# Linear attention and a gated MLP on one core: the heads of a pair on the two partition halves, v padded with zeros

## The chip, the cores and the metric

One core of a Trainium2 chip runs the whole program in one launch. The metric is device time in microseconds (us). An engine's instructions run in the order in which they stand in its own queue; the engines wait for each other through semaphores.

## The reference

For each of 4 sequences and 8 heads a state of 48 x 48 numbers is carried over 768 steps; the output of the heads, side by side, goes through a gated MLP whose gate mixes over time.

```python
for t in range(S):
    cur = einsum('bhd,bhe->bhde', u * k[t], v[t])
    y[t] = einsum('bhd,bhde->bhe', r[t], state + cur)
    state = w * state + einsum('bhd,bhe->bhde', k[t], v[t])
h = relu(x @ w_in);  u, v = h[..., :512], h[..., 512:]
v_s = einsum('ts,bsd->btd', w_spatial, layernorm(v)) + b_spatial
out = (u * v_s) @ w_out
```

## The kernel before, in words

**Attention.** A sequence is cut into 6 chunks of 128 steps, 24 chunks in all, numbered m. Inside a chunk the recurrence becomes matrix products: scores k x r (masked so that a step sees only earlier ones, with the u term on the diagonal) times v, plus the state at the chunk's start times r. A chunk has two halves of 64 steps, z = 0 and 1, each with its own decay reference, so the state is carried from half to half. The 8 heads form 4 pairs p of two heads j.

- `load_chunk` (L84) issues two loads on SP's queue: `rk` (r and k with the head dimension on the partitions, 64 for each head of a pair, L90) and `rkv` (r, k and v with time on the partitions, L94). In `rkv` v has 64 columns for each head, 48 of them filled. Three buffers of each exist.
- `prep` (L236) scales: `scale` (L247, L248, L250) multiplies r and k by powers of w, `rku` (L253, L254) forms r k u, `ks` (L257) scales k with the table `tn`, `red` (L260) sums r k u over a head, `dia` (L269) writes these sums onto the diagonal of the chunk's score tile `a`.
- `g1` (L278) on TensorE: for each head and half, k x r into the PSUM tile `ps` (L286, 16 matmuls with 64 rows and 64 columns), then k x v (L295, 16 such matmuls, 48 wide; 8 ahead of the last chunk of a sequence, since only the first half's is needed there). `ps` has two banks. The row half from which a matmul reads decides its bank.
- `mid` (L305): VectorE copies the scores into `a` under the mask (L309) and carries the state on (L317, L322, L324, L325); ScalarE copies the state into block-diagonal tiles `sb`, 128 rows for a pair of heads (L302, L303).
- `g2` (L328) on TensorE into `xp`: state x r as 12 matmuls for each half (24 in all, 12 in a sequence's first chunk), each with 128 rows of contraction and 32 columns, cycling over the four groups of 32 output partitions; then a x v as 32 matmuls with 64 rows and 32 columns, one for each half, part of a head and output group. All go through `mm` (L335).
- `fin` (L357) splits the result into a high and a low part, `xh` (ScalarE, L365) and `xl` (VectorE, L367).

**MLP.** Each product of the MLP runs as three matmuls of split values (`mm3`, L391 to L393): `moe_v` (L397), `moe_u` (L453), `moe_sp` (L464, the mixing over time), `moe_out` (L478). Weights arrive as 64-bit floats and are unpacked and split by VectorE and ScalarE in small pieces (`from_f64`, lines 182 to 202).

**Order.** Every engine's queue is in the order of the Python code. The main loop runs over chunks i: g2 and fin of chunk i, g1 and mid of chunk i + 1, the loads of chunk i + 3, then `prep` of chunk i + 2 mixed with MLP steps and, in the first chunks, with pieces of weight unpacking (the tables `FIRST` and `POUR` say how many). So TensorE sees for each chunk a dense group of small fp32 matmuls (state x r, a x v, scores, k x v) and then a long run of MLP matmuls. An fp32 matmul of the program appears in the trace as two weight loads and two matmuls, a matmul of the MLP as one of each.

Of the kernel before, what the change touches and what calls it, by code (L numbers as in the profile page):

```python
# [32 lines left out]
ROW = OV + H * 64  # L33
# [3 lines left out]
def fused_kernel(ctx, tc, rkT, rkvN, wT, uB, w_in, w_sp, b_sp, w_out, out):  # L37
# [4 lines left out]
    KPOOL, DACT, VPOOL = 7, 0, 2  # L42
    XPE, SPE = 0, 0
# [89 lines left out]
    mask = const.tile([P, HC], F32, name="mask")  # L133
    nc.gpsimd.memset(mask, 1.0)
    nc.gpsimd.affine_select(out=mask[64:P], in_=mask[64:P], pattern=[[-1, 64]], compare_op=ALU.is_gt,
                            fill=0.0, base=0, channel_multiplier=1)
    nc.gpsimd.affine_select(out=mask[0:64], in_=mask[0:64], pattern=[[1, 64]], compare_op=ALU.is_gt,
                            fill=0.0, base=0, channel_multiplier=-1)
    nc.scalar.mul(neg, eye, -1.0)
    mask_u = mask.bitcast(U32)  # L140
    tn = const.tile([P, NP, 2, D], F32, name="tn")
# [4 lines left out]
    tn_f = tn.rearrange("s p j d -> s (p j d)")  # L146
# [59 lines left out]
    rests = []  # L206

    def sp_pieces(t, j):
        def f():
            if t * NS + j < SPE:  # L210
                hi, lo = (w[:, j, t * TH:(t + 1) * TH] for w in (ws_h, ws_l))
                pm = ps_m.tile([P, 512], F32, name="pm")[:, 0:TH]
                nc.tensor.matmul(pm, eye, raws["sp", t, j], start=True, stop=False)
                nc.scalar.copy(hi, raws["sp", t, j])

                def rest():
                    nc.tensor.matmul(pm, neg, hi, start=False, stop=True)
                    nc.scalar.copy(lo, pm)

                rests.append(rest)  # L220
                if len(rests) > 1:
                    rests.pop(0)()
                if j == NS - 1 or t * NS + j == SPE - 1:
                    rests.pop(0)()
                return
# [10 lines left out]
    def prep(m):  # L236

        rk, rkv = dmas.pop(m)
        rn, kn = rkv[:, 0:DM], rkv[:, OK:OK + DM]
# [4 lines left out]

        def scale():
            if m < KPOOL:
                nc.gpsimd.tensor_tensor(out=rk[:, 1], in0=rk[:, 1], in1=tt, op=ALU.mult)  # L247
# [4 lines left out]
        def rku():
            nc.gpsimd.tensor_tensor(out=rn, in0=rn, in1=kn, op=ALU.mult)  # L253
            nc.gpsimd.tensor_tensor(out=rn, in0=rn, in1=ub, op=ALU.mult)  # L254

        def ks():
            nc.gpsimd.tensor_tensor(out=kn, in0=kn, in1=tn_f, op=ALU.mult)  # L257

        def red():
            nc.vector.tensor_reduce(out=dg.rearrange("s j p -> s p j"),  # L260
                                    in_=rn.rearrange("s (p j d) -> s p j d", p=NP, j=2), axis=AX.X, op=ALU.add)

        def dia():
            if m < DACT:
                for j in range(2):
                    for p in range(NP):
                        nc.scalar.mul(a[:, j, p, :], diag, dg[:, j, p:p + 1])
            else:
                nc.gpsimd.tensor_tensor(out=a.rearrange("s j p t -> s (j p) t"),  # L269
                                        in0=diag.unsqueeze(1).to_broadcast([P, H, HC]),  # L270
                                        in1=dg.rearrange("s j p -> s (j p)").unsqueeze(2).to_broadcast([P, H, HC]),
                                        op=ALU.mult)
# [5 lines left out]
    def g1(m):  # L278
        t = at[m]
        ps = ps_a.tile([P, 2, 512], F32, name="ps")  # L280
        t["ps"] = ps
        for p in range(NP):
            for j in range(2):
                for z, s0, t0 in SUBS:
                    hd = slice(64 * j, 64 * j + 64)
                    nc.tensor.matmul(ps[s0:s0 + 64, j, p * HC:(p + 1) * HC], t["k"][hd, p, s0:s0 + 64],  # L286
                                     t["r"][hd, p, t0:t0 + 64], start=True, stop=True, skip_group_check=True)
        for p in range(NP):
            for j in range(2):
                for z, s0, t0 in SUBS:  # L290
                    if z == 1 and m % NC == NC - 1:
                        continue
                    h = 2 * p + j
                    e0 = 0 if j == 0 else 16
                    nc.tensor.matmul(ps[64 * j:64 * j + 64, s0 // 64, 256 + p * D:256 + (p + 1) * D],  # L295
                                     t["kn"][s0:s0 + 64, h * D:h * D + 64], t["v"][s0:s0 + 64, h, e0:e0 + D],
                                     start=True, stop=True, skip_group_check=True)
# [7 lines left out]
    def mid(m):  # L305
        t, c = at[m], m % NC
        ps = t["ps"]
        ua, ub_ = (ps[:, i, 256:256 + NP * D].rearrange("p (n e) -> p n e", n=NP) for i in (1, 0))
        nc.vector.copy_predicated(out=t["a"], mask=mask_u.unsqueeze(1).unsqueeze(1).to_broadcast([P, 2, NP, HC]),  # L309
                                  data=ps[:, :, 0:256].rearrange("s j (p t) -> s j p t", p=NP))  # L310
        if c == 0:
            block(sblk[1], ua)
            t1 = ua
        else:
# [2 lines left out]
            nc.vector.tensor_tensor(out=t1, in0=st["s"], in1=ua, op=ALU.add)  # L317
            block(sblk[1], t1)
        if c < NC - 1:
            if c == 0:  # L320
                t1 = sm.tile([P, NP, D], F32, name="t1", bufs=1)
# [4 lines left out]
            st["s"] = s2

    def g2(m):  # L328
# [5 lines left out]
        def mm(z, g, jt, lhsT, rhs):  # L334
            nc.tensor.matmul(xp[32 * g:32 * g + 32, z, jt * HC:(jt + 1) * HC], lhsT, rhs, start=(z, g) not in began,  # L335
                             stop=True, skip_group_check=True, tile_position=(ROWP[0], 32 * g))
# [9 lines left out]
        parts = []  # L346
        for jt, g, p, k in quads:
            if k < 2:
                parts.append((jt, g, p, 0, 32 * k))
            if k > 0:  # L350
                parts.append((jt, g, p, 1, 32 * (k - 1)))
        for jt, g, p, j, e in parts:
            for z, s0, t0 in SUBS:
                ROWP[0] = s0
                mm(z, g, jt, t["v"][s0:s0 + 64, 2 * p + j, e:e + 32], t["a"][s0:s0 + 64, j, p, :])

    def fin(m):  # L357
# [11 lines left out]
        return xs, xl, xh, src

    def fin_low(m, xl, xh, src):

        if m < XPE:
            for z in range(2):
                nc.tensor.matmul(src[:, z], neg, xh[:, z], start=False, stop=True, skip_group_check=True)
            nc.scalar.copy(xl, src)

# [253 lines left out]
```

## Time and profile before

| what | value |
|---|---|
| median of 3 runs | 379.26 us (378.18 to 381.27) |
| profiled execution: its own time is the span from first to last instruction | 378.2 us, 1.1 us below the median |
| mean granted TensorE clock | 0.973 |
| TensorE matmul busy | 337.6 us (89%), 5436 instructions |
| weight loads busy | 311.0 us (82%), 5436 instructions |
| VectorE / ScalarE / GpSimd busy | 212.1 / 140.7 / 158.9 us |
| DMA | 41.67 MB |

In the profile PE is TensorE's matmul, PEld its weight load, DVE VectorE, ACT ScalarE, POOL GpSimd and SP the queue that issues the loads. A row of a timeline has the start, the time, the engine, the line, the operation, output <- input, the shapes, how many instructions are merged, and in brackets how long the engine was idle before and what ended that. A row of a group has its busy time, the mean of one in ns, and the idle time before. A row of waits has the total, the number of times and the longest. A row of stretches has the length and then each engine's busy time with its number of instructions, the clock, the DMA share and GB/s. "issue" is a wait for nothing that the profile shows. Matmuls overlap, so their busy time is longer than what they cost; the distance from start to start is what one costs.

### The profile page before, as it was taken

The numbers are of one execution on the slowest core, as the hardware profiler recorded it, in microseconds if no ns is written. First come the engines' busy times: TensorE is split into PE (matmuls) and PEld (weight loads), VectorE is DVE, ScalarE is ACT, GpSimd is POOL, SyncE is SP. The second block draws the span as 40 slices with busy tenths as digits, with TensorE's granted clock in tenths as the row PEclk, the third lists the DMA queues.
The fourth block names the chain that finished last, engine by engine and source line by source line (L and its number), as shares of the span: only waits on it lengthen the run. The fifth ranks groups of instructions, "written<-read, shape, count | busy, mean of one in ns | idle before, by whom it ended". The sixth has DMA issues, their size and how long they took to land.

```text
span 378.2 us, 12232 instructions
## 1 busy us (share of the span) xinstructions
PE 337.6 (89%) x5436; PEld 311.0 (82%) x5436; DVE 212.1 (56%) x419; ACT 140.7 (37%) x310; POOL 158.9 (42%) x162
## 2 busy tenths in 40 slices
PE   2456693997999998998999899999999999999995
PEld 1445472886999997988989899889999998999994
DVE  6698997598655444384444444587444533443120
ACT  3036125747213323647123223547123334461212
POOL 6764854844345271564643263241554330003120
PEclk9996987898999999999999999999999999999999
DMA  7994932450304314323214214333032010000101
GB/s 260 416 390 149 340 103 92 141 178 21 129 2 157 126 74 154 127 67 127 65 35 157 94 56 171 127 117 127 13 110 83 3 44 23 2 0 2 42 21 62
DMA packets 14020, 41.67 MB, mean 110 GB/s; under 512 B 1680, under 2 KB 6416, under 8 KB 13968
## 3 DMA queue, kind: packets, MB, share of 16 engines
q1 hardware_dynamic: 13968, 40.90, 30.7%
q8 instruction: 42, 0.69, 0.8%
q14 instruction: 10, 0.08, 0.1%
HBM read 36.18 MB, written 4.72 MB: 108 GB/s over the span
## 4 chain that ended last, share of the span: by engine, by line
PE 75%; DVE 11%; ACT 4%; DMA 3%; issue 3%; POOL 2%; SPq 0%; POOLq 0%; ACTq 0%; DVEq 0%
PE pm L391 21%; PE pm L393 20%; PE pm L392 20%; PE xp L335 8%; PE ps L286 3%; PE ps L295 2%; DMA wst<-w_sp 2%; DMA rkv<-rkvN 2%; DVE a L309 1%; DVE rk L248 1%; ACT vs L435 1%; DVE q L412 1%; DVE pm L198 1%; DVE pm L194 1%; ACT vnorm L437 1%
## 5 line engine op out<-in xcount | busy, mean ns | idle before, releaser
L473 POOL TENSOR_TENSOR g<-g,u 128x384 f32<-128x384 f32 x32 | 32.6, 1018 | 118.5 <-DVE g L472 118.5
L391 PE MATMUL pm<-ws_h,vnorm 128*128 128x384 f32 x192 | 64.9, 338 | 0.0
L393 PE MATMUL pm<-ws_h,vnorm 128*128 128x384 f32 x192 | 64.3, 335 | 0.0
L392 PE MATMUL pm<-ws_l,vnorm 128*128 128x384 f32 x192 | 64.2, 334 | 0.0
L269 POOL TENSOR_TENSOR a<-diag,dg 128x512 f32<-128x512 f32 x24 | 25.6, 1067 | 67.6 <-DVE dg L260 40.8
L172 DVE TENSOR_TENSOR gt<-g,gt 128x384 fp32r<-128x384 f32 x32 | 20.9, 654 | 58.2 <-ACT gt L171 58.2
L171 ACT CAST gt<-g 128x384 fp32r<-128x384 f32 x32 | 16.4, 514 | 90.5 <-POOL g L473 90.5
L393 PE MATMUL pm<-xh,wi_l 128*128 128x384 f32 x96 | 33.7, 351 | 5.0 <-DVE wi_l L202 5.0
L391 PE MATMUL pm<-xh,wi_h 128*128 128x384 f32 x96 | 34.3, 358 | 3.6 <-ACT u L461 2.4
L391 PEld LDWEIGHTS pm<-ws_h,vnorm 128*128 128x128 f32 x192 | 36.0, 188 | 0.3
L392 PEld LDWEIGHTS pm<-ws_l,vnorm 128*128 128x128 f32 x192 | 36.0, 188 | 0.0
L393 PEld LDWEIGHTS pm<-ws_h,vnorm 128*128 128x128 f32 x192 | 36.0, 188 | 0.0
L391 PE MATMUL pm<-wo_h,gt 128*128 128x384 f32 x96 | 33.0, 344 | 0.8 <-ACT gt L171 0.8
L392 PE MATMUL pm<-xl,wi_h 128*128 128x384 f32 x96 | 33.3, 347 | 0.0
L393 PE MATMUL pm<-wo_h,gt 128*128 128x384 f32 x96 | 32.4, 337 | 0.0
L392 PE MATMUL pm<-wo_l,gt 128*128 128x384 f32 x96 | 32.3, 336 | 0.0
L335 PEld LDWEIGHTS xp<-rk,sb 128*32 128x32 f32 x1056 | 18.0, 115 | 16.4 <-issue 8.4
L335 PE MATMUL xp<-rk,sb 128*32 128x64 f32 x1056 | 23.4, 232 | 8.7 <-DVE xl L367 6.3
L391 PE MATMUL pm<-wi_h,xh 128*128 128x512 f32 x72 | 29.7, 412 | 0.6 <-DVE wi_l L202 0.6
L472 DVE TENSOR_TENSOR g<-pm,bb 128x384 f32<-128x384 f32 x32 | 17.7, 553 | 21.3 <-PE pm L393 21.2
L392 PE MATMUL pm<-wi_l,xh 128*128 128x512 f32 x72 | 29.0, 403 | 0.0
L393 PE MATMUL pm<-wi_h,xl 128*128 128x512 f32 x72 | 28.7, 398 | 0.0
(87 smaller groups left out, 691.9 us busy)
## 6 DMA issues: line engine op xcount, KB each, us to landing
rkv<-rkvN SPq DMA_DIRECT2D x24, 648.0 KB, 5.7
rk<-rkT SPq DMA_DIRECT2D x24, 512.0 KB, 4.3
out<-ob SPq DMA_DIRECT2D x24, 192.0 KB, 1.9
raw<-w_in SPq DMA_DIRECT2D x6, 512.0 KB, 9.9
wst<-w_sp SPq DMA_DIRECT2D x12, 192.0 KB, 5.9
raw<-w_out SPq DMA_DIRECT2D x4, 384.0 KB, 6.9
bb<-b_sp SPq DMA_DIRECT2D x1, 384.0 KB, 5.6
ub<-uB SPq DMA_DIRECT2D x1, 192.0 KB, 6.6
```

Of the source, the lines that this page charges most:

```text
L171: nc.scalar.copy(hi, src)
L172: (eng or nc.vector).tensor_tensor(out=lo, in0=src, in1=hi.bitcast(F32), op=ALU.subtract)
L194: nc.vector.scalar_tensor_tensor(out=z["w"], in0=raws[key][:, :, 0], scalar=2.0 ** -52, in1=z["w"], op0=ALU.mult, op1=ALU.mult)
L269: nc.gpsimd.tensor_tensor(out=a.rearrange("s j p t -> s (j p) t"), in0=diag.unsqueeze(1).to_broadcast([P, H, HC]), in1=dg.rearrange("s j p ...
L286: nc.tensor.matmul(ps[s0:s0 + 64, j, p * HC:(p + 1) * HC], t["k"][hd, p, s0:s0 + 64], t["r"][hd, p, t0:t0 + 64], start=True, stop=True, sk ...
L295: nc.tensor.matmul(ps[64 * j:64 * j + 64, s0 // 64, 256 + p * D:256 + (p + 1) * D], t["kn"][s0:s0 + 64, h * D:h * D + 64], t["v"][s0:s0 + ...
L335: nc.tensor.matmul(xp[32 * g:32 * g + 32, z, jt * HC:(jt + 1) * HC], lhsT, rhs, start=(z, g) not in began, stop=True, skip_group_check=Tru ...
L391: nc.tensor.matmul(o, lh, rh, start=first, stop=False)
L392: nc.tensor.matmul(o, lh, rl, start=False, stop=False)
L393: nc.tensor.matmul(o, ll, rh, start=False, stop=last)
L472: nc.vector.tensor_tensor(out=g, in0=pm[:, 0:TH], in1=bb[:, ts_], op=ALU.add)
L473: nc.gpsimd.tensor_tensor(out=g, in0=g, in1=u, op=ALU.mult)
```

## The change

- The two heads of a pair no longer share the partitions of `ps` and `a`: one head's scores lie on partitions 0 to 63, the other's on 64 to 127, for both time halves z. Which head lies on which half alternates with p (`j ^ b`, b = p // 2), so that in each partition half the two row halves write to different banks.
- v is loaded once for each time half, with 96 columns for a pair; in the rows of a head, the columns of the other head are zeros. `rkv` grows from 1296 to 1552 floats on each partition, 648 to 776 KB.
- a x v becomes, for each half z, 12 matmuls with 128 rows and 32 columns over both heads of a pair: 24 in place of 32.
- `g1` has the same number of matmuls with the same shapes, in another order and at other places of `ps`.
- The mask, the table `tn`, the reduction, the diagonal, the copies and the state's walk through `ps` follow the new layout; `tn` is made by 16 matmuls of 64x48 in place of 4 transposes, the mask by four selections in place of two; `eye` moves into a scratch tile, and `neg`, which only unused branches read, is gone with these (their switches, `XPE`, `SPE` and `DACT`, were 0).

```diff
-ROW = OV + H * 64
+VB = 2 * D
+ROW = OV + 2 * NP * VB
...
-    eye = const.tile([P, P], F32, name="eye")
-    neg = const.tile([P, P], F32R, name="neg")
+    eye = tmp[:, 384:384 + P]
...
-    mask = const.tile([P, HC], F32, name="mask")
+    mask = const.tile([P, 2, HC], F32, name="mask")
...
+    for hf in range(2):
+        for z, sign in ((0, -1), (1, 1)):
+            m_ = mask[64 * hf:64 * hf + 64, z]
+            nc.gpsimd.affine_select(out=m_, in_=m_, pattern=[[sign, 64]], compare_op=ALU.is_gt,
+                                    fill=0.0, base=0, channel_multiplier=-sign)
...
-        nc.tensor.transpose(pt[:, 0:P], tt[:, p, :], eye)
-        nc.scalar.copy(tn[:, p, :, :], pt[:, 0:P].rearrange("s (j d) -> s j d", j=2)[:, :, 0:D])
+        for z, p2, hf in ((z, p2, hf) for z in range(2) for p2 in range(2) for hf in range(2)):
...
+            nc.tensor.matmul(pt[64 * hf:64 * hf + 64, (2 * p2 + z) * D:(2 * p2 + z + 1) * D],
+                             tt[hd, 2 * b + p2, c0:c0 + 64], eye[hd, 64 * j:64 * j + D], start=True, stop=True,
+                             skip_group_check=True)
+        nc.scalar.copy(tn[:, b], pt[:, 0:4 * D])
...
-        for p in range(NP):
-            for j in range(2):
-                for z, s0, t0 in SUBS:
-                    hd = slice(64 * j, 64 * j + 64)
-                    nc.tensor.matmul(ps[s0:s0 + 64, j, p * HC:(p + 1) * HC], t["k"][hd, p, s0:s0 + 64],
-                                     t["r"][hd, p, t0:t0 + 64], start=True, stop=True, skip_group_check=True)
...
-                    nc.tensor.matmul(ps[64 * j:64 * j + 64, s0 // 64, 256 + p * D:256 + (p + 1) * D],
-                                     t["kn"][s0:s0 + 64, h * D:h * D + 64], t["v"][s0:s0 + 64, h, e0:e0 + D],
-                                     start=True, stop=True, skip_group_check=True)
+        quad = [(p2, z, s0, t0, j, b) for p2 in range(2) for z, s0, t0 in SUBS for b in range(2) for j in range(2)]
+        for p2, z, s0, t0, j, b in quad:
+            hd, hf, p, o = slice(64 * j, 64 * j + 64), j ^ b, 2 * b + p2, (2 * p2 + z) * HC
+            nc.tensor.matmul(ps[64 * hf:64 * hf + 64, b, o:o + HC], t["k"][hd, p, s0:s0 + 64],
+                             t["r"][hd, p, t0:t0 + 64], start=True, stop=True, skip_group_check=True)
+        for p2, z, s0, t0, j, b in quad:
+            if z == 1 and m % NC == NC - 1:
+                continue
+            hs, p, o = slice(64 * (j ^ b), 64 * (j ^ b) + 64), 2 * b + p2, 256 + (2 * z + p2) * D
+            kc = (4 * b + 2 * p2 + z) * D
+            nc.tensor.matmul(ps[64 * j:64 * j + 64, b, o:o + D], t["kn"][hs, kc:kc + 64],
+                             t["v"][hs, z, p, j * D:(j + 1) * D], start=True, stop=True, skip_group_check=True)
...
-        nc.vector.copy_predicated(out=t["a"], mask=mask_u.unsqueeze(1).unsqueeze(1).to_broadcast([P, 2, NP, HC]),
-                                  data=ps[:, :, 0:256].rearrange("s j (p t) -> s j p t", p=NP))
+        nc.vector.copy_predicated(out=t["a"].rearrange("s b q z t -> s (b q) (z t)"),
+                                  mask=mask_u.rearrange("s z t -> s (z t)").unsqueeze(1).to_broadcast([P, 4, P]),
+                                  data=ps[:, :, 0:256].rearrange("s b (q c) -> s b q c", q=2))
...
-        parts = []
-        for jt, g, p, k in quads:
-            if k < 2:
-                parts.append((jt, g, p, 0, 32 * k))
-            if k > 0:
-                parts.append((jt, g, p, 1, 32 * (k - 1)))
-        for jt, g, p, j, e in parts:
-            for z, s0, t0 in SUBS:
-                ROWP[0] = s0
-                mm(z, g, jt, t["v"][s0:s0 + 64, 2 * p + j, e:e + 32], t["a"][s0:s0 + 64, j, p, :])
+        for z in range(2):
+            for jt, g, p, k in quads:
+                mm(z, g, jt, t["v"][:, z, p, 32 * k:32 * k + 32], t["a"][:, p // 2, p % 2, z, :])
```

More of the change, by code (lines that the diff above doesn't have):

```diff
@@ L41, in fused_kernel @@
         ctx.enter_context(tc.manual_schedule(engines={e}))
-    KPOOL, DACT, VPOOL = 7, 0, 2
-    XPE, SPE = 0, 0
+    KPOOL, VPOOL = 7, 2
     FIRST = [0, 0, 1, 3, 6, 10]
@@ L132, in fused_kernel @@
     nc.gpsimd.tensor_tensor(out=diag, in0=eye[:, 0:64], in1=eye[:, 64:P], op=ALU.add)
-    mask = const.tile([P, HC], F32, name="mask")
+    mask = const.tile([P, 2, HC], F32, name="mask")
     nc.gpsimd.memset(mask, 1.0)
[L135 to L139, printed above, removed]
+    for hf in range(2):
[3 more added lines that the diff above has]
+                                    fill=0.0, base=0, channel_multiplier=-sign)
     mask_u = mask.bitcast(U32)
-    tn = const.tile([P, NP, 2, D], F32, name="tn")
-    for p in range(NP):
+    tn = const.tile([P, 2, 2 * 2 * D], F32, name="tn")
+    for b in range(2):
         pt = ps_m.tile([P, 512], F32, name="pm")
-        nc.tensor.transpose(pt[:, 0:P], tt[:, p, :], eye)
-        nc.scalar.copy(tn[:, p, :, :], pt[:, 0:P].rearrange("s (j d) -> s j d", j=2)[:, :, 0:D])
-    tn_f = tn.rearrange("s p j d -> s (p j d)")
+        for z, p2, hf in ((z, p2, hf) for z in range(2) for p2 in range(2) for hf in range(2)):
+            j = hf ^ b
+            hd = slice(64 * j, 64 * j + 64)
+            c0 = 64 if z == 0 else 0
+            nc.tensor.matmul(pt[64 * hf:64 * hf + 64, (2 * p2 + z) * D:(2 * p2 + z + 1) * D],
+                             tt[hd, 2 * b + p2, c0:c0 + 64], eye[hd, 64 * j:64 * j + D], start=True, stop=True,
+                             skip_group_check=True)
+        nc.scalar.copy(tn[:, b], pt[:, 0:4 * D])
+    tn_f = tn.rearrange("s b c -> s (b c)")
     atiles = []
     for n in range(2):
-        t = const.tile([P, 2, NP, HC], F32, name=f"a{n}")
+        t = const.tile([P, 2, 2, 2, HC], F32, name=f"a{n}")
         nc.gpsimd.memset(t, 0.0)
@@ L204, in from_f64 @@
         return [first, high, power, low, add, rest]
-    rests = []
     def sp_pieces(t, j):
         def f():
[L210 to L225, printed above, removed]
             split(ws_h[:, j, t * TH:(t + 1) * TH], ws_l[:, j, t * TH:(t + 1) * TH], raws["sp", t, j])
@@ L240, in prep @@
         a = atiles[m % 2]
-        dg = sm.tile([P, 2, NP], F32, name="dg")
+        dg = sm.tile([P, H], F32, name="dg")
         at[m] = dict(r=rk[:, 0], k=rk[:, 1], kn=rkv[:, OK:OK + DM + 16],
-                     v=rkv[:, OV:ROW].rearrange("s (h e) -> s h e", h=H), a=a)
+                     v=rkv[:, OV:ROW].rearrange("s (z p e) -> s z p e", z=2, p=NP), a=a)
         def scale():
@@ L259, in red @@
         def red():
-            nc.vector.tensor_reduce(out=dg.rearrange("s j p -> s p j"),
-                                    in_=rn.rearrange("s (p j d) -> s p j d", p=NP, j=2), axis=AX.X, op=ALU.add)
+            nc.vector.tensor_reduce(out=dg, in_=rn.rearrange("s (h d) -> s h d", h=H), axis=AX.X, op=ALU.add)
         def dia():
-            if m < DACT:
-                for j in range(2):
[L266 to L272, printed above, removed]
+            nc.gpsimd.tensor_tensor(out=a.rearrange("s b q z t -> s (b q z) t"),
+                                    in0=diag.unsqueeze(1).to_broadcast([P, H, HC]),
+                                    in1=dg.unsqueeze(2).to_broadcast([P, H, HC]), op=ALU.mult)
         return [scale, lambda: (rku(), ks()), red, dia]
@@ L281, in g1 @@
         t["ps"] = ps
-        for p in range(NP):
-            for j in range(2):
-                for z, s0, t0 in SUBS:
-                    hd = slice(64 * j, 64 * j + 64)
-                    nc.tensor.matmul(ps[s0:s0 + 64, j, p * HC:(p + 1) * HC], t["k"][hd, p, s0:s0 + 64],
-                                     t["r"][hd, p, t0:t0 + 64], start=True, stop=True, skip_group_check=True)
-        for p in range(NP):
-            for j in range(2):
-                for z, s0, t0 in SUBS:
[L291 to L295, printed above, removed]
-                                     t["kn"][s0:s0 + 64, h * D:h * D + 64], t["v"][s0:s0 + 64, h, e0:e0 + D],
-                                     start=True, stop=True, skip_group_check=True)
+        quad = [(p2, z, s0, t0, j, b) for p2 in range(2) for z, s0, t0 in SUBS for b in range(2) for j in range(2)]
[10 more added lines that the diff above has]
+                             t["v"][hs, z, p, j * D:(j + 1) * D], start=True, stop=True, skip_group_check=True)
     st = {}
     def block(dst, src):
-        nc.scalar.copy(dst[0:64, :, 0:D], src[0:64])
-        nc.scalar.copy(dst[64:P, :, D:2 * D], src[64:P])
+        d4 = dst.rearrange("p (b q) e -> p b q e", b=2)
+        nc.scalar.copy(d4[0:64, :, :, 0:D], src[0:64])
+        nc.scalar.copy(d4[64:P, :, :, D:2 * D], src[64:P])
     def mid(m):
@@ L307, in mid @@
         ps = t["ps"]
-        ua, ub_ = (ps[:, i, 256:256 + NP * D].rearrange("p (n e) -> p n e", n=NP) for i in (1, 0))
-        nc.vector.copy_predicated(out=t["a"], mask=mask_u.unsqueeze(1).unsqueeze(1).to_broadcast([P, 2, NP, HC]),
-                                  data=ps[:, :, 0:256].rearrange("s j (p t) -> s j p t", p=NP))
+        ua, ub_ = (ps[:, :, 256 + z * 2 * D:256 + (z + 1) * 2 * D].rearrange("p b (q e) -> p b q e", q=2)
+                   for z in range(2))
+        nc.vector.copy_predicated(out=t["a"].rearrange("s b q z t -> s (b q) (z t)"),
+                                  mask=mask_u.rearrange("s z t -> s (z t)").unsqueeze(1).to_broadcast([P, 4, P]),
+                                  data=ps[:, :, 0:256].rearrange("s b (q c) -> s b q c", q=2))
         if c == 0:
@@ L315, in mid @@
             block(sblk[0], st["s"])
-            t1 = sm.tile([P, NP, D], F32, name="t1", bufs=1)
+            t1 = sm.tile([P, 2, 2, D], F32, name="t1", bufs=1)
             nc.vector.tensor_tensor(out=t1, in0=st["s"], in1=ua, op=ALU.add)
@@ L320, in mid @@
             if c == 0:
-                t1 = sm.tile([P, NP, D], F32, name="t1", bufs=1)
+                t1 = sm.tile([P, 2, 2, D], F32, name="t1", bufs=1)
                 nc.vector.tensor_copy(out=t1, in_=ua)
-            s2 = sm.tile([P, NP, D], F32, name="s2")
+            s2 = sm.tile([P, 2, 2, D], F32, name="s2")
             nc.vector.tensor_tensor(out=s2, in0=t1, in1=ub_, op=ALU.add)
-            nc.vector.tensor_tensor(out=s2, in0=s2, in1=w128.unsqueeze(2).to_broadcast([P, NP, D]), op=ALU.mult)
+            nc.vector.tensor_tensor(out=s2, in0=s2, in1=w128.rearrange("p (b q) -> p b q", b=2).unsqueeze(3).to_broadcast([P, 2, 2, D]), op=ALU.mult)
             st["s"] = s2
@@ L335, in mm @@
             nc.tensor.matmul(xp[32 * g:32 * g + 32, z, jt * HC:(jt + 1) * HC], lhsT, rhs, start=(z, g) not in began,
-                             stop=True, skip_group_check=True, tile_position=(ROWP[0], 32 * g))
+                             stop=True, skip_group_check=True, tile_position=(0, 32 * g))
             began.add((z, g))
         quads = [(jt, g, *((jt, g) if g < 3 else (3, jt))) for jt in range(NK) for g in range(4)]
-        ROWP = [0]
         for z, s0, t0 in SUBS:
@@ L365, in fin @@
         nc.scalar.copy(xh, src)
-        if m >= XPE:
-            nc.vector.tensor_tensor(out=xl, in0=src, in1=xh.bitcast(F32), op=ALU.subtract)
+        nc.vector.tensor_tensor(out=xl, in0=src, in1=xh.bitcast(F32), op=ALU.subtract)
         del at[m]
[L369 to L376, printed above, removed]
+        return xs
     due, now = {}, [0]
@@ L595, in dmajor, with pairs @@
         return t.reshape(B, NC, P, NP, C)
+    heads = [[2 * p + (hf ^ (p // 2)) for p in range(NP)] for hf in range(2)]
     def tmajor(a):
-        a = a.reshape(B, H, NC, C, D)[:, :, :, s_order]
-        return np.ascontiguousarray(a.transpose(0, 2, 3, 1, 4)).reshape(B, NC, C, DM)
-    rkvN = np.zeros((B, NC, C, ROW), r.dtype)
-    rkvN[..., 0:DM] = tmajor(r)
-    rkvN[..., OK:OK + DM] = tmajor(k)
-    vp = rkvN[..., OV:ROW].reshape(B, NC, C, NP, 2, 64)
-    tv = tmajor(v).reshape(B, NC, C, NP, 2, D)
-    vp[..., 0, 0:D] = tv[..., 0, :]
-    vp[..., 1, 16:64] = tv[..., 1, :]
-    rkvN[..., OV:ROW] = vp.reshape(B, NC, C, H * 64)
+        a = a.reshape(B, H, NC, C, D)[:, :, :, t_order].reshape(B, H, NC, 2, 64, D)
+        a = np.stack([a[:, hs] for hs in heads], 1)
+        return a.transpose(0, 3, 1, 5, 4, 2, 6)
+    def pairs(a):
+        a = tmajor(a).reshape(B, NC, C, 2, 2, 2, D)
+        return a.transpose(0, 1, 2, 4, 5, 3, 6).reshape(B, NC, C, DM)
+    rkvN = np.zeros((B, NC, C, ROW), r.dtype)
+    rkvN[..., 0:DM] = pairs(r)
+    rkvN[..., OK:OK + DM] = pairs(k)
+    vp = np.zeros((B, NC, 2, 64, 2, NP, 2, D), v.dtype)
+    tv = tmajor(v)
+    for hf in range(2):
+        for p in range(NP):
+            vp[:, :, hf, :, :, p, hf ^ (p // 2)] = tv[:, :, hf, :, :, p]
+    rkvN[..., OV:ROW] = vp.reshape(B, NC, C, ROW - OV)
+    ub = np.stack([np.repeat(u[hs], 2, 0).reshape(DM) for hs in heads])
     wt = np.ones((2, 64, NP), w.dtype)
@@ L616 @@
         "wT": wt.reshape(P, NP),
-        "uB": np.ascontiguousarray(np.broadcast_to(u.reshape(1, DM), (P, DM))),
+        "uB": np.repeat(ub, 64, 0),
         "w_in": np.ascontiguousarray(moe_w_in[np.concatenate(rows)]).view(np.int64),
```

5 lines of the change are left out of this document (1 added, 4 removed).

## The prediction, made before the changed kernel ran

> **What bounds the kernel now.** I read the busy times by stretch first, then the waits of TensorE, then the timeline of its weight loads around one chunk, and last the stops that the profile puts down to nobody. Busy time by stretch:
>
> ```profile
> core 0: us, PE busy (x) PEld busy (x) DVE busy (x) ACT busy (x) POOL busy (x), PEclk, DMA share, GB/s
> 24.00:62.00 38.00, 26.37 (x711) 20.72 (x700) 34.72 (x69) 13.98 (x35) 22.55 (x22) 0.86 0.61 213
> 62.00:93.00 31.00, 26.26 (x418) 23.25 (x419) 24.80 (x52) 19.70 (x41) 15.41 (x14) 0.85 0.34 105
> 93.00:320.00 227.00, 222.35 (x3780) 207.96 (x3778) 118.53 (x234) 82.90 (x187) 95.64 (x92) 1.00 0.27 91
> ```
>
> There are two stages. Up to 62 us VectorE is busy 34.7 of 38 us (it unpacks the weights), so there TensorE waits for it; from 93 us on TensorE is busy 222 of 227 us and no other engine more than 118.5. What TensorE does from 93 us on counts fully, what it does before counts little. Its waits from 93 us to the end, matmuls and then weight loads, and its short fp32 groups in the same stretch:
>
> ```profile
> PE ps L295 <- issue: 4.6, 4, 1.6
> PE pm L391 <- ACT gt L171: 0.8, 1, 0.8
> PEld ps L295 <- issue: 5.1, 4, 1.7
> L335 PE MATMUL xp<-a,rkv 64*32 64x64 f32 x1088 | 16.5, 223 | 0.0
> L335 PE MATMUL xp<-rk,sb 128*32 128x64 f32 x768 | 14.2, 221 | 0.0
> L295 PE MATMUL ps<-rkv 64*64 64x48 f32 x464 | 11.3, 217 | 4.6 <-issue 4.6
> L286 PE MATMUL ps<-rk 64*64 64x64 f32 x512 | 11.1, 224 | 0.0
> ```
>
> One fp32 matmul of the program is two here (two passes, each a weight load and a matmul). 1088 / 64 = 17 chunks lie behind 93 us. The means overlap, so I take times from the distance of starts. The weight loads of a usual chunk, of the start of a sequence's first chunk, and of a chunk before a sequence's last:
>
> ```profile
> 127.52 0.72 PEld L335 LDWEIGHTS xp<-rk,sb 128*32 128x32 f32 x48 [0.25 <-DVE gt L172]
> 128.33 0.81 PEld L335 LDWEIGHTS xp<-a,rkv 64*32 64x32 f32 x64
> 129.24 0.56 PEld L286 LDWEIGHTS ps<-rk 64*64 64x64 f32 x32
> 129.70 0.56 PEld L295 LDWEIGHTS ps<-rkv 64*64 64x64 f32 x32
> 130.31 0.19 PEld L391 LDWEIGHTS pm<-ws_h,vnorm 128*128 128x128 f32 x1
> 130.60 0.19 PEld L393 LDWEIGHTS pm<-ws_h,vnorm 128*128 128x128 f32 x1
> 130.78 0.19 PEld L391 LDWEIGHTS pm<-ws_h,vnorm 128*128 128x128 f32 x1
> 166.46 0.38 PEld L335 LDWEIGHTS xp<-rk,sb 128*32 128x32 f32 x24 [0.36 <-issue]
> 166.94 0.81 PEld L335 LDWEIGHTS xp<-a,rkv 64*32 64x32 f32 x64
> 308.15 0.55 PEld L295 LDWEIGHTS ps<-rkv 64*64 64x64 f32 x16
> 308.76 0.19 PEld L391 LDWEIGHTS pm<-wo_h,gt 128*128 128x128 f32 x1
> ```
>
> So a chunk is a burst of 2.79 us (127.52 to 130.31): state x r 0.81, a x v 0.91, scores 0.46, k x v 0.61. Each change of tile shape shows as about 0.1 us without a weight load (128.24 to 128.33, 129.14 to 129.24).
>
> **a x v.** 24 loads of 128x32 take 0.48 us, 48 take 0.81: 0.33 / 24 = 13.75 ns each, and 0.15 us that does not grow with their number. The new a x v is 24 matmuls, 48 loads, of just this shape, behind others of this shape with no change between: 96 x 13.75 ns + 0.15 = 1.47 us for both, against 0.81 + 0.91 = 1.72. It saves 0.25 us a chunk, 17 times: **4.25 us**. From below: had each new load the whole 0.81 / 48 = 16.9 ns, 0.10 a chunk (1.7 us); from above: the 11.1 ns of the old loads ((0.81 - 0.11) / 63), 0.38 (6.4 us). I take the middle, because shape and rotation over the four column groups are those of the state's matmuls.
>
> **k x v of a last chunk.** 16 loads (308.15 to 308.76) take the 0.61 us that 32 take: the first form uses one row half alone there. The new order alternates the row halves in every pair, so I expect 16 x 13.4 ns = 0.21 less, 3 times (464 = 13 x 32 + 3 x 16): **0.63 us**, between 0 and 0.8.
>
> **Scores and k x v otherwise**: same shapes, the four 64x64 tiles in another rotation, and now both row halves write into the same bank of ps at once, each into its own 64 partitions. No row of before shows two row halves in one bank. Bounds: 11.1 ns a load as above (a gain of 0.2 us a chunk, 3.3 in all) and the one-row-half rate of 308.15 (a loss of 0.9 a chunk, a rival below). I take zero: four tiles remain in turn, as at 129.24.
>
> **The four stops.** The weight loads break off inside k x v. The page's instruction counts, one of the four stops, the packet of the instruction queue between 141.6 and 142.8 us, the page's count of such packets, and the instructions between one restart and the next:
>
> ```profile
> PE 337.6 (89%) x5436; PEld 311.0 (82%) x5436; DVE 212.1 (56%) x419; ACT 140.7 (37%) x310; POOL 158.9 (42%) x162
> 142.07 0.32 PEld L295 LDWEIGHTS ps<-rkv 64*64 64x64 f32 x7
> 144.11 0.36 PEld L295 LDWEIGHTS ps<-rkv 64*64 64x64 f32 x9 [1.73 <-issue]
> q8 instruction: 1, 0.02, 5.0%
> q8 instruction: 42, 0.69, 0.8%
> 144.10:179.36 35.26, 34.15 (x637) 30.63 (x636) 18.71 (x43) 19.26 (x40) 15.77 (x14) 1.00 0.32 111
> 179.36:199.06 19.70, 18.70 (x255) 18.09 (x255) 9.18 (x17) 4.09 (x11) 11.17 (x12) 1.00 0.20 59
> 199.06:215.87 16.81, 15.86 (x254) 15.25 (x254) 6.82 (x13) 4.74 (x12) 5.28 (x6) 1.00 0.33 109
> ```
>
> 0.69 MB over TensorE's 5436 loads and 5436 matmuls is 63 bytes each, so a packet is a block of about 256. Between restarts stand 637 + 636, 255 + 255 and 254 + 254 instructions: with the few that only wait and are not counted, 5, 2 and 2 blocks. The stops are refills of TensorE's instructions, and sit at every boundary of a block that falls badly. Counting the order of before, all four lie 194 past a multiple of 256. A burst runs its 352 in 2.79 us, 8 ns each, the MoE about 90 ns each (130.60 to 130.78 is a pair); the packet goes out 1.3 to 2.5 us ahead of the restart at 144.11. Some 2 us are covered as long as MoE instructions are still queued ahead of the boundary. So a boundary bites where it lies late in a burst: counted from the burst's start, the four are at 302, 319, 333 and 342; boundaries at 209 to 256 show no stop and one at 295 almost none.
>
> The change takes 8 matmuls of four instructions out of every chunk and so moves all later boundaries. On TensorE (xp is the output of state x r and a x v, ps of scores and k x v, a_161 and a_168 the same buffer) a usual chunk stands before as
>
> ```order
> L335 MATMUL xp<-rk,sb_163 32x64 x12
> L335 MATMUL xp<-rk,sb_165 32x64 x12
> L335 MATMUL xp<-a_161,rkv 32x64 x32
> L286 MATMUL ps<-rk 64x64 x16
> L295 MATMUL ps<-rkv 64x48 x16
> L391 MATMUL pm<-ws_h,vnorm 128x384
> ```
>
> and now as
>
> ```order
> L314 MATMUL xp<-rk,sb_170 32x64 x12
> L314 MATMUL xp<-rk,sb_172 32x64 x12
> L314 MATMUL xp<-a_168,rkv 32x64 x24
> L265 MATMUL ps<-rk 64x64 x16
> L272 MATMUL ps<-rkv 64x48 x16
> L353 MATMUL pm<-ws_h,vnorm 128x384
> ```
>
> Nothing else moved: the neighbours are the same, a x v has 24 rows for 32. Bursts are now 321 to 323 long (289 before a sequence's last chunk, 274 at its first). Counted through the changed order with the same 194, the boundaries from 93 us on lie at 11 to 267 in their bursts, or behind a burst's end (281 of 274, 310 of 289 and later); none between 295 and an end. I expect no stop: the 5.1 us of idle loading, and 0.13 more for each, since a load lasts 0.15 us and the next normally starts 14 ns behind it: **5.6 us**, between 0 and that.
>
> The Trainium skill (Runtime: NRT & Kernel Launch, Instruction fetch mechanics) has the same blocks of 256 instructions, but says that crossing a boundary is mostly hidden because dispatch is slower than the fill. The four idle rows disagree within a burst and agree outside. By the rule the stops have another cause, and a sum without the 5.6 is a rival below.
>
> **The first 93 us.** A chunk's rkv has 256 more floats per partition, since v comes with zeros: 128 KB more. The rate while loads queue, and what waits for the first:
>
> ```profile
> GB/s 260 416 390 149 340 103 92 141 178 21 129 2 157 126 74 154 127 67 127 65 35 157 94 56 171 127 117 127 13 110 83 3 44 23 2 0 2 42 21 62
> 5.42 1.77 POOL L247 TENSOR_TENSOR rk<-rk,tt 128x512 f32<-128x512 f32 x1 [1.26 <-DMA rk<-rkT]
> 8.79 1.00 POOL L253 TENSOR_TENSOR rkv<-rkv 128x384 f32<-128x384 f32 x1 [1.61 <-DMA rkv<-rkvN]
> 10.82 1.00 POOL L257 TENSOR_TENSOR rkv<-rkv,tn 128x384 f32<-128x384 f32 x1
> 10.90 0.55 DVE L260 TENSOR_REDUCE dg<-rkv 128x8 f32<-128x384 f32 x1 [1.19 <-POOL rkv L254]
> 2.28 0.23 POOL L137 TENSOR_SCALAR_AFFINE_SELECT mask<-mask 64x64 f32<-64x64 f32 x1
> 31.80 0.74 DVE L309 COPY_PREDICATED a<-mask,ps 128x512 f32<-128x512 uint32 x1
> 32.43 0.34 DVE L317 TENSOR_TENSOR t<-s,ps 128x192 f32<-128x192 f32 x1
> ```
>
> ```order
> L90 DMA rk<-rkT 128x1024
> L68 DMA raw<-w_in 128x1024
> L94 DMA rkv<-rkvN 128x1552
> L102 DMA ub<-uB 128x384
> L90 DMA rk<-rkT 128x1024
> ```
>
> On SP's queue rkv, formerly 128x1296, is still third behind wt. 131 KB at 416 GB/s is 0.32 us, which POOL (L253 waits for this load), then VectorE (L260), then the whole unpacking inherit: **+0.3 us**; up to 1.3 if the first four loads all count, 0 if TensorE's shorter chunks give it back. POOL's two more masks, 0.23 us each, go into its 1.26 us of idle time ahead of L247; tn is wanted by L257 at 10.82 only. Uncovered, either were about 0.5 us. copy_predicated, the sums into s and the copies into sb keep their element counts, with another walk through ps: nothing behind 93 us, where VectorE idles half the time; before, should they take 10% more, 7 chunks x (0.74 + 2 x 0.34) x 0.1 = 1.0 us.
>
> **Sum** against the profiled execution: 378.2 - 4.25 - 0.63 - 5.6 + 0.3 = 368.0. Its span lies 1.1 under the median of the runs (379.26), so 369.1 in these terms; I say **369.0 us**.
>
> **Rivals.**
> - *The stops stay or move.* For it: the 194 is counted from before, and what stands ahead of the first instruction of the program isn't shown. Against: the multiples of 256. All staying gives 369.1 + 5.6 = 374.7. Chance 0.14.
> - *Two row halves in one bank take turns* in scores and k x v: slower. For it: before, each row half writes only its own bank; k x v of a last chunk shows the rate with half the tiles, 0.61 us for 16 loads. Then the scores and k x v, 0.46 + 0.61 less 0.15 for changes of shape, double: 0.92 x 16 chunks (512 / 32) = 14.7, and the 0.63 is lost: 384.4. It decides from about 10 ns more per load (10 us over 1024). Against: they write different partitions. Chance 0.10. The Trainium skill (TensorEngine Tiling (Array Packing), Gotcha 1: PSUM Pressure) says that different row tiles cannot access one bank at a time, without regard to partitions; no row of before tests it.
> - *The start grows* by 3 to 5 us, because VectorE reads ps more slowly across two banks: about 373. Chance 0.07.
> - *Nothing shows*, since another engine takes over behind 93 us: about 379. VectorE's 118.5 of 227 us speaks against it. Chance 0.05.
>
> **How the numbers follow.** The forecast has 0.64, its own range 366 to 372. For 8 in 10 I add the case of staying stops at the top and faster 64x64 tiles (11.1 ns) at the bottom: 365 to 375.5. A measurement here tells about 1% from no change, 375.5 to 383: faster 0.64 + 0.11 + 0.07 = 0.82, same 0.03 + 0.05 = 0.08, slower 0.10.
>
> **What would show it.** Right: from 93 us on, 0.66 us from the first a x v load to the end of that group without a gap ahead of it, a burst of 2.54 us instead of 2.79, 2.33 before a last chunk, no issue wait in k x v. Wrong: a scores group over 0.6 us, an issue wait of 1 us anywhere in a burst, VectorE's first TENSOR_REDUCE more than 0.5 us later than 10.90.

## The result and the profile after

| | before | after |
|---|---|---|
| median of 4 runs | 378.98 us (378.18 to 381.27) | 369.49 us (369.19 to 371.25) |
| ratio after / before | | 0.975, 95% interval 0.972 to 0.979 |
| span of the profiled execution | 378.2 us | 367.9 us |

The change is faster by 2.5%. The forecast was 369.0 us, in a range of 365 to 375.5, and 368.0 for the span.

Where the time went shows in the busy time by stretch, cut at the start of the burst in which TensorE becomes the bound. Before:

```profile
62.00:93.41 31.41, 26.67 (x419) 23.41 (x419) 25.14 (x53) 20.11 (x41) 15.82 (x14) 0.85 0.33 103
93.41:378.20 284.79, 276.06 (x4075) 259.76 (x4074) 135.46 (x270) 101.31 (x221) 103.40 (x100) 1.00 0.22 77
```

After (columns as there: length, then PE, PEld, DVE, ACT and POOL busy with their counts, clock, DMA share, GB/s):

```profile
62.00:93.69 31.69, 26.14 (x387) 22.96 (x388) 25.07 (x53) 19.84 (x41) 15.52 (x14) 0.89 0.33 110
93.69:367.90 274.21, 270.10 (x3803) 255.90 (x3802) 135.22 (x270) 101.24 (x221) 103.59 (x100) 1.00 0.24 87
```

The same work behind this burst takes 284.79 us before and 274.21 after, 10.6 us less; VectorE, ScalarE and POOL do the same number of instructions in the same time. The start is 0.3 us longer. TensorE loses 272 matmuls of the trace: 17 chunks x 16, two for each of the 8 that a x v has fewer.

One chunk after the change, by its weight loads up to the first of the MLP; then three rows of a chunk ahead of a sequence's last (its first row, its k x v, and the first of the MLP):

```profile
127.32 0.71 PEld L314 LDWEIGHTS xp<-rk,sb 128*32 128x32 f32 x48 [0.25 <-DVE gt L177]
127.96 0.74 PEld L314 LDWEIGHTS xp<-a,rkv 128*32 128x32 f32 x48
128.79 0.56 PEld L265 LDWEIGHTS ps<-rk 64*64 64x64 f32 x32
129.25 0.56 PEld L272 LDWEIGHTS ps<-rkv 64*64 64x64 f32 x32
129.87 0.19 PEld L353 LDWEIGHTS pm<-ws_h,vnorm 128*128 128x128 f32 x1
296.47 0.72 PEld L314 LDWEIGHTS xp<-rk,sb 128*32 128x32 f32 x48 [0.25 <-issue]
298.41 0.33 PEld L272 LDWEIGHTS ps<-rkv 64*64 64x64 f32 x16
298.79 0.19 PEld L353 LDWEIGHTS pm<-wo_h,gt 128*128 128x128 f32 x1
```

State x r now takes 0.64 us to the start of a x v, where it took 0.81: the pause for a change of shape is gone. a x v takes 0.83 in place of 0.91. Both together are 1.47, as forecast. Scores and k x v have the old 0.46 and 0.62. The burst is 2.55 us in place of 2.79, and 2.32 ahead of a last chunk, where 16 loads of k x v now take 0.38 us and not 0.61.

The waits of TensorE's matmuls from 93 us on, and those of its weight loads that stand under "issue":

```profile
PE pm L353 <- ACT gt L176: 0.8, 1, 0.8
PEld xp L314 <- issue: 2.7, 10, 0.4
```

There is no wait in k x v any more: the 5.1 us in four stops are gone. What remains under "issue" is the 0.25 to 0.36 us ahead of a burst, as before. The traces also show what stood behind the four stops. Before, a 16 KB packet of the instruction queue starts at 141.72, 176.69, 196.75 and 213.44 us, 2.3 to 2.7 us ahead of each of the four restarts. After, counted in the same way, no boundary of a block behind 93 us comes less than 3.0 us behind its packet.

### The profile page after: what moved, and what is told of

It is laid out like the page before. It is cut to its first block, busy times and chain, and to the rows that moved or that the text cites. A ratio compares the mean times of both kernels' runs of the same rounds, so it can differ in the third digit from the quotient of the medians.

```text
span 367.9 us, 11518 instructions
## 1 busy us (share of the span) xinstructions
PE 331.6 (90%) x5080; PEld 307.9 (84%) x5080; DVE 212.8 (58%) x419; ACT 139.9 (38%) x307; POOL 158.7 (43%) x164
## 4 chain that ended last, share of the span: by engine, by line
PE 76%; DVE 15%; ACT 3%; issue 2%; DMA 2%; POOL 1%; SPq 0%; POOLq 0%; DVEq 0%; ACTq 0%
PE pm L353 22%; PE pm L355 21%; PE pm L354 21%; PE xp L314 7%; PE ps L265 3%; PE ps L272 2%; DMA rkv<-rkvN 2%; DVE rk L235 2%; DVE a L287 2%; DVE pm L187 1%; DVE ws_l L177 1%; DVE pm L203 1%; DVE q L374 1%; DVE pm L199 1%; DVE wi_l L207 1%
## 5 line engine op out<-in xcount | busy, mean ns | idle before, releaser
L314 PE MATMUL xp<-rk,sb 128*32 128x64 f32 x1056 | 23.4, 232 | 10.5 <-DVE xl L337 7.8
L353 PE MATMUL pm<-wi_h,xh 128*128 128x512 f32 x72 | 30.6, 425 | 2.3 <-DVE wi_l L207 2.3
L354 PE MATMUL pm<-wi_l,xh 128*128 128x512 f32 x72 | 29.8, 414 | 0.0
L355 PE MATMUL pm<-wi_h,xl 128*128 128x512 f32 x72 | 29.6, 411 | 0.0
L337 DVE TENSOR_TENSOR xl<-xp,xh 128x384 fp32r<-128x384 f32 x24 | 13.2, 552 | 25.2 <-ACT xh L336 25.2
```

Of the source, the lines that this page charges most:

```text
L353: nc.tensor.matmul(o, lh, rh, start=first, stop=False)
L354: nc.tensor.matmul(o, lh, rl, start=False, stop=False)
L355: nc.tensor.matmul(o, ll, rh, start=False, stop=last)
```

## The experiments

The theory: of the 10.6 us, about 4 come from state x r and a x v in one shape, 0.7 from k x v ahead of last chunks, and nearly 6 from four refills (fetches of the next block of 256 of TensorE's instructions) that fell late in a burst and now don't. The rivals: the stops belonged to what stands at their place in the code; a x v gained by its fewer matmuls, with shapes changing for free; matmuls are paid by their number alone. All times below stand beside runs of the kernel before on the same chip (379.2 us); the changed kernel was not run again beside them, and its 369.49 us is that of the table above. Burst times are distances from its first weight load to the first of the MLP.

**e1: the kernel before, its boundaries moved by 212 instructions.**

```diff
         pt = ps_m.tile([P, 512], F32, name="pm")
+        if p == 0:
+            for _ in range(53):
+                nc.tensor.matmul(pt[0:32, 256:288], eye[:, 0:32], eye[:, 0:32], start=True, stop=True,
+                                 skip_group_check=True)
         nc.tensor.transpose(pt[:, 0:P], tt[:, p, :], eye)
```

> The kernel before with 53 extra fp32 matmuls (212 instructions, results unused) on TensorE in the first 5 us, where it idles; nothing else differs. Theory (the four stops in k x v are refills at every 256th instruction, and bite only late in a burst): all boundaries lie 212 earlier in their bursts, the four stops vanish, at most two others remain at about 300 of a burst with under 2 us together; bursts stay 2.79 us; time 379.0 - 5.8 + (0.5 to 2) = 373.7 to 375.2 us. Rival (the stops come from what stands at that place, such as a wait or the loads issued there): the same four stops, 379 us.

Measured: 376.69 us (374.93 to 378.51), ratio 0.994 (0.991 to 0.996). The profiled execution is the fastest of eight, with a span of 373.2 us. Its waits on issue behind 93 us, weight loads:

```profile
PEld xp L339 <- issue: 3.0, 11, 0.4
PEld ps L299 <- issue: 0.8, 1, 0.8
PEld pm L397 <- issue: 0.2, 1, 0.2
```

The four stops are gone from a kernel that does not have the change; one came at 300 of the burst at 93.2 us (0.95 us longer than 2.79), one touched the MLP behind a burst (0.2 us). From the burst at 93.2 us on it takes 280.0 us (93.22 to 373.2), against 284.8. So the stops follow the boundaries, not the code. The median is 1.5 us over what I expected; what the other executions lost isn't in the profile.

For the first 24 us the profile gives a granted clock of 0.75 here and of 1.00 before. That does not mean that TensorE was slower here. The loads of the first scores, before and then in e1:

```profile
7.24 0.95 PEld L286 LDWEIGHTS ps<-rk 64*64 64x64 f32 x32 [1.26 <-POOL rk L247]
7.19 0.59 PEld L290 LDWEIGHTS ps<-rk 64*64 64x64 f32 x32 [0.28 <-issue]
```

The same 32 loads take 0.95 us before, although the clock is given as 1.00, and 0.59 in e1. The trace of before has its first record of the clock at 27.17 us, that of e1 at 5.32 us, and time without a record is counted as 1.00. So the two figures can't be compared.

**e2: the changed kernel, moved by 148 instructions** (37 such matmuls at the same place).

> The changed kernel with 37 such extra matmuls (148 instructions) in the first 5 us. Theory: six boundaries come to lie at 299 to 332 of a burst, so stops come back, four to six of 0.3 to 1.5 us, 3.5 to 7 us in all: 373 to 376.5 us; the bursts without one stay 2.56 us. Rival (the new layout took the cause of the stops away): no stop, 369.5 us.

Measured: 376.36 us (373.72 to 376.9). The profiled span is 374.5. One of its bursts:

```profile
192.70 0.71 PEld L318 LDWEIGHTS xp<-rk,sb 128*32 128x32 f32 x48 [0.25 <-issue]
193.34 0.74 PEld L318 LDWEIGHTS xp<-a,rkv 128*32 128x32 f32 x48
194.17 0.56 PEld L269 LDWEIGHTS ps<-rk 64*64 64x64 f32 x32
194.63 0.54 PEld L276 LDWEIGHTS ps<-rkv 64*64 64x64 f32 x26
196.49 0.20 PEld L276 LDWEIGHTS ps<-rkv 64*64 64x64 f32 x6 [1.31 <-issue]
196.75 0.19 PEld L357 LDWEIGHTS pm<-wo_h,gt 128*128 128x128 f32 x1
```

The stop is back inside the new layout: 4.05 us for the burst, 1.49 more than 2.56. Four bursts have one, with their boundaries at 299, 308, 312 and 321: 0.83, 1.49, 1.08 and 1.45, 4.9 us in all. The two boundaries at 330 and 332 lie just behind the end of their bursts (321 to 323 instructions). One costs nothing; at the other the loads stop for 0.53 us among the first of the MLP, and the way to the next burst is 15.75 us in place of the 15.26 after the change. The start, up to 94.97, grew by 1.3 us.

**e3: the changed kernel with 8 repeats in a x v, and moved back to the old places.**

```diff
             for jt, g, p, k in quads:
                 mm(z, g, jt, t["v"][:, z, p, 32 * k:32 * k + 32], t["a"][:, p // 2, p % 2, z, :])
+                if g == 3 or jt == 0 and g == 0:
+                    nc.tensor.matmul(xp[32 * g:32 * g + 32, z, 256:256 + HC], t["v"][:, z, p, 32 * k:32 * k + 32],
+                                     t["a"][:, p // 2, p % 2, z, :], start=True, stop=True, skip_group_check=True,
+                                     tile_position=(0, 32 * g))
```

The 50 extra matmuls at the start are not printed; they stand where e2 has its 37. The start flag of the repeats resets sums of xp in their bank, so the numbers computed are others; only the times are read.

> The changed kernel with 8 more 128x32 matmuls in each a x v (repeats into unused columns of the PSUM tile, 32 matmuls as before the change), and 50 extra matmuls at the start, so that every instruction behind 93 us has the place in its block of 256 that it had before the change. Theory: 16 x 13.3 ns = 0.21 us more per burst (2.77), 3.6 in all, and the same four stops at the same places in k x v, 5.8 us: 369.5 + 9.4 = 378.9 us. Rival for the stops (the new layout took their cause away): 373.1 us. Rival for a x v (its gain came from the number of matmuls, not from the change of shape): bursts of 2.79 as before.

Measured: 384.13 us (382.68 to 386.19). The stops came as expected, in the same four bursts, at 303, 343, 320 and 334, but short: 1.9 us of idle loading in all.

```profile
PEld xp L318 <- issue: 3.0, 11, 0.4
PEld ps L276 <- issue: 1.9, 4, 0.5
```

The price of the repeats was wrong: a burst took 3.25 us, 0.69 more, 43 ns for each load. Each repeat goes to the column group (32 output partitions) of the matmul just ahead of it, and seems to wait for it; e7 asks this. The start flag is not what costs: in a sequence's first chunk after the change the first four matmuls of a x v carry it too, and a x v takes 0.83 us as elsewhere. Three of the stops are 0.6 to 0.7 us shorter than before, as much as the burst is longer: a refill takes as long as ever (2.3 to 2.4 us from the packet to the restart), and more of it is covered. The first, 0.58 us for 1.85, shrank by more: its packet starts 1.03 us into the burst, where it started 1.84 us into it before. Why it goes out earlier isn't shown.

**e7: the 8 repeats in turn over the column groups**, no shift, with start=False.

```diff
+            for jt, g, p, k in quads[0:4]:
+                nc.tensor.matmul(xp[32 * g:32 * g + 32, z, 256:256 + HC], t["v"][:, z, p, 32 * k:32 * k + 32],
+                                 t["a"][:, p // 2, p % 2, z, :], start=False, stop=True, skip_group_check=True,
+                                 tile_position=(0, 32 * g))
```

> The changed kernel with 8 more 128x32 matmuls in each a x v, two rounds over the four column groups in turn (sums into unused columns), no other extra. Theory (a load in this shape costs 13.3 ns when the column groups take turns): 16 x 13.3 = 0.21 us per burst, 2.77 in place of 2.56, 3.6 us in all; boundaries come to lie at 341 and 349 of two bursts (1.2 to 1.4 us each), at 332 and 363 of two more (0 to 1 us each): 369.5 + 3.6 + (2.4 to 4.5) = 375.5 to 377.6 us. Rival (in this shape a load costs 43 ns, as the repeats placed right behind a matmul of their own column group did): bursts of 3.25 us.

Measured: 377.27 us (376.19 to 380.3). A burst without a stop (L328 are the repeats):

```profile
129.46 0.71 PEld L314 LDWEIGHTS xp<-rk,sb 128*32 128x32 f32 x48 [0.25 <-DVE gt L177]
130.10 0.41 PEld L314 LDWEIGHTS xp<-a,rkv 128*32 128x32 f32 x24
130.43 0.19 PEld L328 LDWEIGHTS xp<-a,rkv 128*32 128x32 f32 x8
130.54 0.41 PEld L314 LDWEIGHTS xp<-a,rkv 128*32 128x32 f32 x24
130.88 0.19 PEld L328 LDWEIGHTS xp<-a,rkv 128*32 128x32 f32 x8
131.16 0.56 PEld L265 LDWEIGHTS ps<-rk 64*64 64x64 f32 x32
131.62 0.56 PEld L272 LDWEIGHTS ps<-rkv 64*64 64x64 f32 x32
132.24 0.19 PEld L357 LDWEIGHTS pm<-ws_h,vnorm 128*128 128x128 f32 x1
```

2.78 us: 16 more loads cost 0.22, 13.9 ns each, in this shape and in turn. The two stops came at 341 and 349, 1.09 and 1.23 us; the boundaries at 332 (burst of 321) and 363 cost nothing within a burst, but behind the second the loads of the MLP stop for 0.53 us. The start, to 95.38 us, took 1.7 us more than after the change.

**e4: one matmul of a x v in the shape 64x32.**

```diff
-                mm(z, g, jt, t["v"][:, z, p, 32 * k:32 * k + 32], t["a"][:, p // 2, p % 2, z, :])
+                n = 64 if z == 0 and (jt, g) == (0, 0) else P
+                mm(z, g, jt, t["v"][0:n, z, p, 32 * k:32 * k + 32], t["a"][0:n, p // 2, p % 2, z, :])
```

> The changed kernel; the first of the 24 matmuls of a x v takes its 64 rows that are not zeros, so its shape is 64x32 among 128x32: as many matmuls, two more changes of shape per chunk, no instruction moved. Theory (a change of shape costs 0.1 to 0.17 us of TensorE): 0.2 to 0.34 us per burst, 3.4 to 5.8 in all: 373 to 375.3 us, no stop. Rival (shapes change for free, the gain of a x v was its fewer matmuls): 369.5 us, bursts of 2.56.

Measured: 375.58 us (374.95 to 375.93), no stop in k x v.

```profile
127.94 0.72 PEld L314 LDWEIGHTS xp<-rk,sb 128*32 128x32 f32 x48 [0.25 <-DVE gt L177]
128.75 0.94 PEld L314 LDWEIGHTS xp<-a,rkv 64*32 64x32 f32 x48
129.78 0.56 PEld L265 LDWEIGHTS ps<-rk 64*64 64x64 f32 x32
130.24 0.56 PEld L272 LDWEIGHTS ps<-rkv 64*64 64x64 f32 x32
130.86 0.19 PEld L354 LDWEIGHTS pm<-ws_h,vnorm 128*128 128x128 f32 x1
```

State x r takes 0.81 us again and a x v 1.03: 2.91 or 2.92 for the burst, 0.35 more for two changes of shape, 17 times 6 us. A change costs TensorE 0.17 us. That is 0.17 of the 0.24 us that the change gained in a usual chunk; the rest goes with the 16 loads fewer.

**e6: the kernel before, with all of k x v ahead of a last chunk too** (the `continue` for z == 1 is gone).

> The kernel before, which now also makes k x v of the second half ahead of a sequence's last chunk (8 more matmuls, results unused). Theory (those 8 sit on the row half that idles there): the burst ahead of a last chunk stays at 2.79 us though it has 32 instructions more; and since later boundaries move, stops come at 309 to 333 of five bursts, 1.2 to 1.8 us each, in place of the four: 379.2 - 5.8 + (6.2 to 8) = 379.6 to 381.4 us. Rival for the term (instructions are paid by their number): bursts of 3.0 us there. Rival for the stops: the same four as before.

Measured: 380.52 us (379.88 to 383.54), ratio 1.004 (1.001 to 1.007). The end of the burst ahead of a last chunk, and the waits on issue:

```profile
142.15 0.56 PEld L286 LDWEIGHTS ps<-rk 64*64 64x64 f32 x32
142.61 0.56 PEld L293 LDWEIGHTS ps<-rkv 64*64 64x64 f32 x32
143.23 0.19 PEld L389 LDWEIGHTS pm<-wo_h,gt 128*128 128x128 f32 x1
```

```profile
PEld ps L293 <- issue: 4.6, 5, 1.2
```

32 loads take 0.62 us where 16 took 0.61: those 16 had one row half to themselves. And there are five stops in place of the four, in the five bursts with a boundary at 309 to 333; they lengthen these by 0.87 to 1.41 us, 5.4 in all, less than foreseen. The time falls into the foreseen range only because the start is longer, too: that burst stands at 93.98 us.

**e8: the kernel before, moved by 212 instructions in the burst of chunk 4.**

```diff
+        for n in range(53 if m == 4 else 0):
+            g = n % 4
+            nc.tensor.matmul(xp[32 * g:32 * g + 32, 1, 256:272], sblk[1][:, 0, 0:32], t["r"][:, 0, 0:16],
+                             start=False, stop=True, skip_group_check=True, tile_position=(0, 32 * g))
         parts = []
```

> The kernel before with the 53 extra matmuls (212 instructions) not at the start but in the burst of chunk 4 at about 53 us, 16 columns wide, where VectorE sets the pace. Theory: the stops are as with the same shift at the start (one of about 1 us in the burst at 93 us), and without the earlier start of TensorE the clock of the first stage stays as before, so the time keeps the whole gain: 379.2 - 5.8 + 1 + (0 to 1.4) = 374.4 to 375.8 us. Rival (moving the boundaries is worth only the 2.5 us that the first shift showed): 376.7 us.

Measured: 376.93 us (375.1 to 379.0), ratio 0.993 (0.990 to 0.996): the rival's number. But the profile (span 375.2) shows the two halves apart: from the burst at 95.03 us on it takes 280.2 us, 4.6 less than before, as e1; up to there it takes 1.6 us more than the 93.41 of before. The burst of chunk 5 already starts 1.1 us late (71.15 us for 70.08), behind the extra matmuls and a stop of 2.06 us in the burst that holds them. Then a boundary falls into the burst of chunk 5 itself:

```profile
73.38 0.39 PEld L295 LDWEIGHTS ps<-rkv 64*64 64x64 f32 x19
74.84 0.25 PEld L295 LDWEIGHTS ps<-rkv 64*64 64x64 f32 x9 [1.07 <-issue]
```

It lengthens this burst by 1.20 us, and the next one starts 2.3 us late. e1 has the same stop: its burst of chunk 5 starts 0.9 us early (69.21 us) and takes 1.32 us longer, and the next one starts 0.45 us late. So my claim that nothing in the first 93 us would cost was wrong: near its end, with TensorE 85% busy before, a stop counts whole. From there to the next burst, at 93.22 and 95.03 us, both take 0.65 us less than before, which goes with the clock on that way (see the first 93 us below). The other ground of the expectation, that e1 had slowed the clock of the first stage, does not hold either, as e1's loads show.

## Why the prediction was right

- **a x v, 4.25 us**: 2.79 to 2.55 or 2.56 us for a burst, 17 times, is 4.0. The price per load (13.75 ns foreseen; 0.64 / 48 = 13.3 after, 13.9 in e7) and the pause that goes with a shape (0.15 us foreseen, 0.17 in e4) held. The sign of 0.66 us to the end of the a x v group did not come: its row has 0.74. The 0.66 are 48 prices from start to start, and a row goes on to the end of its last load, which lasts 0.11 us; state x r and a x v together take the 1.47 us of the sum.
- **k x v of a last chunk, 0.63 us**: 0.24 less at each of three, 0.7. e6 bears out the reason, one idle row half: 16 more loads on it took no time.
- **The stops, 5.6 us**: the four bursts were 5.8 us over 2.79, and none is over 2.56 after. e1, e2, e6 and e7 moved the boundaries by other amounts, in both layouts, and the stops went where the count of 256 put them; a boundary that lies from about 300 to the end of a burst bites, by 0.5 to 1.9 us, and one some ten instructions behind the end costs 0 to 0.5 us. In e1, e2, e3, e6 and e7 every restart within a burst comes 2.2 to 2.8 us behind the start of a packet of the instruction queue. The Trainium skill's rule (Runtime: NRT & Kernel Launch, Instruction fetch mechanics), that crossing a boundary is mostly hidden, holds for most of the boundaries here and fails late in the bursts, by those 0.5 to 1.9 us.
- **The first 93 us, +0.3 us**: the sum holds (93.69 for 93.41), the way to it does not. POOL starts on the first rkv at 8.79 us in both, and VectorE's first sum over it at 10.89 for 10.90:

```profile
8.79 0.99 POOL L240 TENSOR_TENSOR rkv<-rkv 128x384 f32<-128x384 f32 x1 [1.92 <-DMA rkv<-rkvN]
10.89 0.55 DVE L247 TENSOR_REDUCE dg<-rkv 128x8 f32<-128x384 f32 x1 [0.69 <-POOL rkv L241]
```

  In the experiments that burst starts anywhere from 92.7 to 95.4 us, so 0.3 can't be told from the scatter of the start. Part of this scatter is the clock. The way from the burst at about 80 us to this one, before and after, with the columns of the stretches above:

```profile
80.32:93.41 13.09, 10.73 (x189) 9.42 (x188) 11.47 (x28) 8.58 (x18) 5.44 (x6) 0.87 0.27 93
81.23:93.69 12.46, 9.30 (x173) 8.26 (x173) 10.85 (x28) 8.32 (x18) 4.89 (x5) 1.00 0.30 107
```

  In e1, e3, e4, e6 and e8 the clock of this way is given as 1.00, too, and it takes 12.42 to 12.60 us; in e2 and e7 the clock is 0.88 and 0.77 and it takes 13.96 and 15.11. So the changed kernel was 0.9 us late at 81.23 us, and 0.6 came back on a way with a better clock than before: that 0.3 came out is luck.
- **The rival of two row halves in one bank**: scores and k x v kept 0.46 and 0.62 us. The starts are those of before, too: four loads within 20 ns, the next four 58 ns behind the first, while one row half alone (the 16 loads at 308.15 us before) has two every 58 ns in the end. So nothing shows row halves that write different partitions of one bank taking turns; the Trainium skill's rule (TensorEngine Tiling (Array Packing), Gotcha 1: PSUM Pressure) is too wide for that case.

Sum behind the start: 4.0 + 0.7 + 5.8 = 10.5 of the 10.6 us.

## What to carry to other kernels

More than half of this gain came from where 256-instruction boundaries fell, not from the work removed: in a stretch of short matmuls, look for waits that nobody caused, count the instructions between them, and expect that any edit that changes the count of TensorE's instructions moves them, for better or worse. A change of tile shape has a price of its own (0.17 us here), so padding with zeros to stay in one shape can pay even when it costs DMA bytes. Small matmuls were fast here only while they took turns over the tiles (13.9 ns a load, against 43 behind one of the own column group).

## What the runs showed of the hardware that I had not expected

- A matmul put right behind one of its own column group costs 43 ns a load, in turn 13.9 (e3, e7).
- The granted clock of a stretch without a record of the clock is given as 1.00, and this can mislead: before, the 32 loads at 7.24 us take 0.95 us at "1.00"; in e1, where TensorE starts 3.8 us earlier, they take 0.59, and in the late burst at 129.24 us 0.56. What an early start is worth isn't settled: e1 reached the burst of chunk 5 0.9 us earlier than before, e2 reached it at 71.00 us for 71.22 after the change.
- Behind the start, bursts of one kind without a stop were the same to 0.06 us within a kernel. The start itself ended between 92.7 and 95.4 us in these kernels, and the latest of them, e2, e7 and e8, are late for different reasons: a clock of 0.88 and 0.77 on the last 14 to 15 us in e2 and e7, extra matmuls and two stops in e8. What sets the clock there isn't shown.
